# Pooled attention with a two-expert feed-forward: new homes for the first batch's small work

## The chip, the cores and the metric

The kernel runs on one core of a Trainium2 chip. The metric is the device time in microseconds of one execution; a profile of one execution shows what each engine did. The engines are called PE (matrix products; PEld is its weight load), DVE (VectorE), ACT (ScalarE), POOL (GpSimd) and SP (the queue that issues nearly all transfers here).

## The reference

```python
# B, H, S, D = 4, 8, 1152, 64
q_pool = q.reshape(B, H, S // 2, 2, D).mean(axis=3)
scores = np.matmul(q_pool, k.transpose(0, 1, 3, 2)) / np.sqrt(D)
scores = scores - np.max(scores, axis=-1, keepdims=True)
attn = np.exp(scores)
attn = attn / (np.sum(attn, axis=-1, keepdims=True) + 1e-09)
x = np.matmul(attn, v)                       # then (B, 576, 512)
xn = (x - mu) / np.sqrt(var + 1e-06) * g_ln  # over the last axis
out = x + np.maximum(xn @ w_ch1, 0.0) @ w_ch2   # w_ch1 512 x 2048, w_ch2 2048 x 512
```

q, k and v are float32. The two weight matrices are float64.

## The kernel before, in words

The attention is cut into 144 steps. A step has 128 rows of pooled queries against the 1152 keys of one head (each fifth of nine holds 64 rows of each of two heads). Nine steps are a pair of heads, four pairs a batch. The order of every engine is the order in which the program is written: the function `step(i)` is called for i = 0, 1, 2, ..., and the calls in it set what stands behind what on each engine.

The first batch (steps 0 to 35, `on_pe(i)`) and the other three go different ways. In the first batch a step is: PE makes the scores of the next step into PSUM (`emit_s`, L372 and L380; two sets of three banks in turn); DVE scales them and finds the row's maximum in one instruction (`emit_max`, L392); ACT takes the exponential (`emit_exp`, L399); PE transposes the 128x1152 result in nine blocks back into the same PSUM banks (`emit_t`, L429); ACT copies it to SBUF in two halves of 512 and 640 columns (`emit_t_copy`, L435). Two steps later PE multiplies it by V in float32 (`emit_pv`, L453): V has a 65th column of ones, so that row 64 of the 65x128 product is the sum of the exponentials. ACT copies that product to SBUF and adds 1e-9 to row 64 (L955), PE turns it back (`emit_turn`, L478), and DVE takes the reciprocal of the sum and scales (L508, L516). In the later batches the exponentials are split in two fp16 halves (ACT, and DVE or POOL in steps 2, 5 and 8 of nine, L410 to L419), transposed by a DMA, and multiplied by V in fp16 (L462); there the feed-forward products of finished batches (L613, L645) run beside the attention.

While the first batch runs, the weights come in. Each of 32 pieces is loaded by a DMA in step m (`w_load`), ACT moves its high words (`w_bias`, L719, step m + 3), and in step m + 4 `w_conv` puts three operations in a list (`fill`) that DVE works off at the step's end: the largest high word (a reduce), the low words shifted right by 29, and the join of both, `(x << 3) | low`. All three are recorded at one line, L105. After each eight pieces a scale is found, and POOL splits each piece pair in fp16 halves in three instructions, one a step (`calm`; L239, L239, L786); from part 2 on they have steps of their own. Before each such instruction stands a `gate`: DVE writes a column (L244) and POOL copies it (L245), so that POOL waits until DVE has come to that place. POOL also pools q and copies V (`take_v`, L261).

Of the kernel before, what the change touches and what calls it, by code (L numbers as in the profile page):

```python
# [12 lines left out]
I32 = mybir.dt.int32  # L13
ACTF = mybir.ActivationFunctionType
# [10 lines left out]
def tile_pooled_attention_moe(  # L25
# [18 lines left out]
    nc = tc.nc  # L44
# [36 lines left out]
    gsb = const.tile([128, KD], FP32, name="gsb")  # L81
    gs1 = const.tile([128, 2, KD], FP32, name="gs1")
    wtop = const.tile([128, 4, KD, 2], FP32, name="wtop")
    ones = const.tile([128, 128], BF16, name="ones")
    diag = const.tile([128, 4, 4], BF16, name="diag")
    wmax = const.tile([128, 4], FP32, name="wmax")
    wexp = const.tile([128, 4], FP32, name="wexp")
    wscl = const.tile([128, 4], FP32, name="wscl")
    inv12 = const.tile([128, 2], FP32, name="inv12")
    nought = const.tile([128, 1], FP32, name="nought")  # L90
    both = const.tile([128, 2], FP32, name="nhalf")
    nhalf, eps = both[:, 0:1], both[0:65, 1:2]
# [154 lines left out]
    def take_v(p, h):  # L247

        st = pair[p]
        vr = raws[p, "v"]  # L250
        if "v" not in st:

            st["v"] = tr_p.tile([128, 2, C, 130], FP16, tag="v", name="vt")
            if on_pe(p * C):
                st["v"] = st["v"].bitcast(FP32)
                nc.gpsimd.memset(st["v"][:, :, :, 64:65], 1.0)
# [140 lines left out]
    def emit_exp(i):  # L397
        st = steps[i]
        nc.scalar.activation(out=st["pe"], in_=st["pe"], func=ACTF.Exp, scale=-1.0, bias=st["nb"])  # L399

    pts = {}
# [70 lines left out]
    def emit_turn(n, ot, i):  # L472

        j = n % C
        ps = psum[:, 3 * ((i if on_pe(i) else pv_slot[0]) % 2) + 2, 128:258]
        parts = [(h, 64 * h, 64) for h in range(2)] if j == 4 else [(0, 0, 128)]
# [8 lines left out]
    def evac_pv(i, ps):  # L485
# [18 lines left out]
        r = r[o:o + n, 0:m] if on_pe(i) else r[:, 0:1]  # L504

        def one():
            if on_pe(i):
                nc.vector.reciprocal(r, ps[o:o + n, 64:65 * m:65])  # L508
            else:
                nc.vector.tensor_scalar(r, ps[:, 64:65], EPS, s, op0=ALU.add, op1=ALU.mult)  # L510
                nc.vector.reciprocal(r, r)

        def two():
            for u in range(m):
                if on_pe(i):
                    nc.vector.tensor_scalar(  # L516
                        x[:, 64 * u:64 * u + 64], ps[o:o + n, 65 * u:65 * u + 64],
                        r[:, u:u + 1], None, op0=ALU.mult,
                    )
                    continue  # L520
                a = slice(64 * u, 64 * u + 64) if m == 2 else slice(0, 128)
# [202 lines left out]
    def w_conv(m):  # L724
# [7 lines left out]
            nc.vector.tensor_reduce, wtop[:, part, c, z:z + 1], hi.bitcast(FP32), axis=AX.X,  # L732
# [3 lines left out]
        later(  # L736
            nc.vector.scalar_tensor_tensor, xi, xi, 3, lo,
            op0=ALU.logical_shift_left, op1=ALU.bitwise_or,
        )

    def w_reduce(part):
        while fill:
            drip()
        x, m = wtop[:, part], wmax[:, part:part + 1]
# [58 lines left out]
    for p in range(1, NP):  # L803
# [142 lines left out]
    def a_piece(i):  # L946
        pieces.extend(ready.pop(i, ()))
        for u in range(2 if len(pieces) > 2 and not on_pe(i) else 1):
            if pieces:
# [14 lines left out]
    def step(i):  # L964
# [73 lines left out]
        if calm and i < HP * C - 1:  # L1038
            gate()
# [10 lines left out]
    with tc.manual_schedule():  # L1050
# [10 lines left out]
        nc.vector.memset(both[:, 1:2], 0.0)  # L1061
        nc.vector.memset(both[64:65, 1:2], 1e-9)
# [5 lines left out]
        make_identity(nc, ident)  # L1068

# [64 lines left out]
```

## Time and profile before

| | |
|---|---|
| median of 3 runs | 813.77 us (811.7 to 814.31) |
| the profiled execution's own time | 812.92 us |
| its span from first to last instruction | 811.1 us |
| busy: PE, DVE, ACT, POOL | 97%, 74%, 67%, 42% of the span |
| TensorE clock granted, mean | 0.998 |

The profiled execution is 0.85 us below the median of the runs. Busy shares are averages over very different stages: the first batch takes some 177 us, and which engine sets the pace changes after it.

### The profile page before, as it was taken

The numbers are of one execution on the slowest core, as the hardware profiler recorded it, in microseconds if no ns is written. First come the engines' busy times: TensorE is split into PE (matmuls) and PEld (weight loads), VectorE is DVE, ScalarE is ACT, GpSimd is POOL, SyncE is SP. The second block draws the span as 40 slices with busy tenths as digits, with TensorE's granted clock in tenths as the row PEclk, the third lists the DMA queues.
The fourth block names the chain that finished last, engine by engine and source line by source line (L and its number), as shares of the span: only waits on it lengthen the run. The fifth ranks groups of instructions, "written<-read, shape, count | busy, mean of one in ns | idle before, by whom it ended". The sixth has DMA issues, their size and how long they took to land.

```text
span 811.1 us, 21365 instructions
## 1 busy us (share of the span) xinstructions
PE 783.1 (97%) x8978; PEld 553.7 (68%) x8978; DVE 599.3 (74%) x1174; ACT 544.4 (67%) x788; POOL 341.3 (42%) x338
## 2 busy tenths in 40 slices
PE   8899999989989999989999999999999999999997
PEld 7688888767556666657566666766675757766764
DVE  4599999999989887898777878888787867522121
ACT  3799898877786878787767776787778676211100
POOL 2010243389999963475452524528252423200000
PEclk9999999999999999999999999999999999999999
DMA  5828464208699999998998989896979687401001
GB/s 146 248 68 286 155 195 142 81 17 157 124 192 158 186 162 206 175 191 156 207 167 180 178 176 172 164 198 116 223 136 209 128 146 123 81 1 27 14 1 27
DMA packets 276017, 115.95 MB, mean 143 GB/s; under 512 B 259280, under 2 KB 259280, under 8 KB 275920
## 3 DMA queue, kind: packets, MB, share of 16 engines
q1 hardware_dynamic: 275840, 114.29, 69.9%
q8 instruction: 70, 1.15, 0.6%
q10 hardware_dynamic: 80, 0.29, 0.2%
q14 instruction: 27, 0.22, 0.1%
HBM read 46.14 MB, written 4.72 MB: 63 GB/s over the span
## 4 chain that ended last, share of the span: by engine, by line
PE 67%; POOL 13%; DVE 10%; issue 4%; ACT 3%; DMA 2%; SPq 0%; POOLq 0%; ACTq 0%; DVEq 0%
PE psum L645 19%; PE psum L613 18%; PE psum L372 8%; PE psum L462 7%; PE psum L453 5%; POOL wsl L239 4%; PE psum L429 3%; POOL wsl L786 3%; PE psum L380 2%; POOL hl L417 2%; DVE pe L392 2%; DVE hl L419 1%; DMA vr<-in_v_dram 1%; PE psum L321 1%; PE psum L1048 1%
## 5 line engine op out<-in xcount | busy, mean ns | idle before, releaser
L392 DVE CUSTOM_DVE_ANT_0 pe<-psum,nought,sc 128x1152 f32<-128x1152 f32 x144 | 203.1, 1411 | 17.5 <-PE psum L462 7.5
L399 ACT ACTIVATE pe<-pe,nb 128x1152 f32<-128x1152 f32 x144 | 180.4, 1253 | 31.9 <-DVE nb L392 31.0
L645 PE MATMUL psum<-wsl,ht 128*128 128x512 f16 x864 | 196.6, 379 | 4.7 <-DVE ht L627 3.8
L613 PEld LDWEIGHTS <-wsl 128*128 128x128 f16 x1920 | 169.6, 98 | 20.9 <-issue 3.2
L613 PE MATMUL psum<-xn,wsl 128*128 128x256 f16 x1536 | 176.3, 273 | 2.9 <-DVE xb L659 1.9
L645 PEld LDWEIGHTS <-ht 128*128 128x128 f16 x864 | 81.2, 98 | 93.0 <-issue 5.0
L626 ACT ACTIVATE ht<-psum 128x512 f16<-128x512 f32 x72 | 42.9, 595 | 129.2 <-PE psum L613 129.0
L410 ACT ACTIVATE hl<-pe 128x1152 f16<-128x1152 f32 x108 | 125.6, 1163 | 3.4
L372 PE MATMUL psum<-kt,qt 64*128 64x512 f16 (+1 forms) x960 | 120.2, 382 | 3.1 <-ACT pt L435 2.3
L419 DVE SCALAR_TENSOR_TENSOR hl<-pe,hl 128x1152 f16<-128x1152 f32 x72 | 116.5, 1618 | 0.0
L462 PE MATMUL psum<-vt,pt 128*128 128x65 f16 (+2 forms) x3240 | 106.8, 194 | 0.1
L627 DVE SCALAR_TENSOR_TENSOR ht<-psum,ht 128x512 f16<-128x512 f32 x72 | 49.6, 689 | 74.4 <-ACT ht L626 74.3
L462 PEld LDWEIGHTS <-pt 128*128 128x128 f16 (+1 forms) x3240 | 98.3, 100 | 3.0 <-DMA pt<-hl 0.3
L239 POOL TENSOR_SCALAR pe<-pe 128x1152 f32<-128x1152 f32 x36 | 42.8, 1189 | 119.3 <-ACT hl L410 119.3
L417 POOL TENSOR_TENSOR hl<-pe,hl 128x1152 f16<-128x1152 f32 x36 | 87.1, 2420 | 3.0
L453 PE MATMUL psum<-pt,vt 128*65 128x128 f32 (+1 forms) x720 | 77.4, 263 | 1.2 <-DVE kt L271 1.2
L453 PEld LDWEIGHTS psum<-pt,vt 128*65 128x65 f32 x720 | 71.4, 138 | 1.6 <-DVE kt L271 1.4
L372 PEld LDWEIGHTS <-qt 64*128 64x128 f16 (+1 forms) x960 | 31.6, 96 | 49.5 <-issue 30.8
L380 PEld LDWEIGHTS <-qt 128*128 128x128 f16 (+1 forms) x320 | 17.1, 99 | 63.1 <-issue 63.1
L245 POOL COPY gate<-gate 128x1 f32<-128x1 f32 x27 | 5.0, 184 | 110.7 <-DVE gate L244 110.7
L271 DVE SCALAR_TENSOR_TENSOR qt<-psum,s,qt 128x512 f16<-128x512 f32 (+1 forms) x48 | 29.4, 614 | 29.3 <-ACT qt L274 29.1
L659 DVE SCALAR_TENSOR_TENSOR xb<-psum,inv,xb 128x512 f32<-128x512 f32 x32 | 23.9, 745 | 36.7 <-PE psum L645 36.5
(114 smaller groups left out, 978.3 us busy)
## 6 DMA issues: line engine op xcount, KB each, us to landing
stage<-in_moe_w_ch_dram SPq DMA_DIRECT2D x32, 512.0 KB, 6.9
kr<-in_k_dram SPq DMA_DIRECT2D x16, 576.0 KB, 4.6
vr<-in_v_dram SPq DMA_DIRECT2D x16, 576.0 KB, 5.2
qr<-in_q_dram SPq DMA_DIRECT2D x31, 288.0 KB, 5.1
out_dram<-xb SPq DMA_DIRECT2D x32, 128.0 KB, 2.4
pt<-hl SPq DMA_TRANSPOSE x108, 5.2
kr<-in_k_dram SPq DMA_DIRECT2D x16, 64.0 KB, 4.2
out_dram<-xh SPq DMA_DIRECT2D x4, 128.0 KB, 2.8
```

The source lines that it names most:

```text
L239: nc.gpsimd.tensor_scalar(dst, src, s, 1.0, op0=ALU.mult, op1=ALU.mult)
L372: nc.tensor.matmul(out=sp[o:o + w, c0:c0 + 512], lhsT=qt[r:r + 64, qa, q0:q0 + w], rhs=kt[r:r + 64, ka, h], start=(a == 0), stop=(a == 2),)
L392: nc.vector.tensor_tensor_reduce(out=st["pe"], in0=st["s"], in1=nought[:, 0:1].to_broadcast([128, S]), scale=pair[i // C]["sc"][:, 0:1], s ...
L399: nc.scalar.activation(out=st["pe"], in_=st["pe"], func=ACTF.Exp, scale=-1.0, bias=st["nb"])
L410: nc.scalar.activation(out=hl[:, 0], in_=st["pe"], func=ACTF.Copy, scale=2.0 ** 15)
L417: nc.gpsimd.tensor_tensor(hl[:, 1], st["pe"], hl[:, 0], op=ALU.subtract)
L419: nc.vector.scalar_tensor_tensor(hl[:, 1], st["pe"], 2.0 ** 15, hl[:, 0], op0=ALU.mult, op1=ALU.subtract)
L453: nc.tensor.matmul(out=ps[0:65, q0:q0 + w], lhsT=vt[:, h, c], rhs=pt[:, 128 * u + q0:128 * u + q0 + w], start=(u == 0), stop=(u == C - 1),)
L462: nc.tensor.matmul(out=dst[:, 0:n], lhsT=pt[:, a + u, q0:q0 + w], rhs=vt[:, h, c, x0:x0 + n], start=(u == 0 and a == 0 and n == 65), stop= ...
L613: nc.tensor.matmul(out=ps[:, o:o + n], lhsT=wsl[:, 8 * w + cc, wa, f * 128:f * 128 + 128], rhs=xn[:, xa * KD + cc, 0:n], start=(m == 0), s ...
L627: lambda: nc.vector.scalar_tensor_tensor(lo, pv, 0.0, hi, op0=ALU.max, op1=ALU.subtract),
L645: nc.tensor.matmul(out=ps, lhsT=hv[0][:, ha, f, t * 128:t * 128 + 128], rhs=wsl[:, 8 * w + 4 + f // 2, wa, (f % 2) * DM:(f % 2) * DM + DM] ...
```

## The change

Four things change, in the first batch alone. The join of the weights' words goes from DVE to POOL, as an integer product by eight and an integer sum (two instructions for one). The product with V drops the column of ones, has 64 columns of weights instead of 65, and puts even and odd key blocks on different halves of PE's columns, so that two 64-row partial products stand one under the other in PSUM; DVE instead of ACT copies all 128 rows; and the turn back is a float32 product with two stacked identities, which adds the halves. The exponential's own instruction gives the row sums, to which POOL adds 1e-9. In every sixth step of the batch DVE copies the second half of the transposed block instead of ACT. The gates go, and the transposes of the next pair's q and k (`a_prep`) stand ahead of the product with V, no longer behind it.

```diff
     def emit_exp(i):
         st = steps[i]
-        nc.scalar.activation(out=st["pe"], in_=st["pe"], func=ACTF.Exp, scale=-1.0, bias=st["nb"])
+        kept = {}
+        if on_pe(i):
+            x = sums[i] = sums8[:, i % 8:i % 8 + 1]
+            kept["accum_out"] = x
+        nc.scalar.activation(
+            out=st["pe"], in_=st["pe"], func=ACTF.Exp, scale=-1.0, bias=st["nb"], **kept
+        )
+        if on_pe(i):
+            nc.gpsimd.tensor_scalar(x, x, 1e-9, 1.0, op0=ALU.add, op1=ALU.mult)
...
         for a, b in ((0, 512), (512, S)):
-            nc.scalar.copy(st["pt"][:, a:b], st["s"][:, a:b])
+            copy = nc.vector.tensor_copy if a and i % 6 == 1 else nc.scalar.copy
+            copy(st["pt"][:, a:b], st["s"][:, a:b])
...
                 for u, c in enumerate(ORDER):
+                    o = 64 * (u % 2)
                     nc.tensor.matmul(
-                        out=ps[0:65, q0:q0 + w], lhsT=vt[:, h, c],
+                        out=ps[o:o + 64, q0:q0 + w], lhsT=vt[:, h, c, 0:D],
                         rhs=pt[:, 128 * u + q0:128 * u + q0 + w],
-                        start=(u == 0), stop=(u == C - 1),
+                        start=(u < 2), stop=(u >= C - 2), skip_group_check=True,
                     )
...
-        for h, q0, w in parts:
-            nc.tensor.transpose(ps[0:w, 65 * h:65 * h + 65], ot[:, q0:q0 + w], ident[0:65, 0:65])
+        for q0, w in ((0, 64), (64, 64)) if j == 4 else ((0, 128),):
+            nc.tensor.matmul(
+                out=ps[q0:q0 + w, 0:D], lhsT=ot[:, q0:q0 + w], rhs=stack, start=True, stop=True,
+                skip_group_check=True,
+            )
...
             if on_pe(i):
-                nc.vector.reciprocal(r, ps[o:o + n, 64:65 * m:65])
+                nc.vector.reciprocal(r, sums.pop(i))
...
-        later(
-            nc.vector.scalar_tensor_tensor, xi, xi, 3, lo,
-            op0=ALU.logical_shift_left, op1=ALU.bitwise_or,
-        )
+        def join():
+
+            nc.gpsimd.tensor_tensor(xu, xu, eight[:, 0:1].to_broadcast([128, 512]), op=ALU.mult)
+            nc.gpsimd.tensor_tensor(xu, xu, lu, op=ALU.add)
+
+        later(join)
...
-            if on_pe(p * C):
-                at(i0 + (5, 7)[n], gate)
...
                 if on_pe(n):
-                    ot = pt.rearrange("p a n -> p (a n)").bitcast(FP32)[0:65, 0:128]
-                    until([lambda ot=ot, ps=ps: nc.scalar.activation(
-                        out=ot, in_=ps[0:65, 0:128], func=ACTF.Identity, bias=eps
-                    )], nbank[1])
+                    ot = pt.rearrange("p a n -> p (a n)").bitcast(FP32)[:, 0:128]
+                    nc.vector.tensor_copy(ot, ps[:, 0:128])
+                    waiting.discard(nbank[1])
...
+            a_prep()
             a_piece(i)
-            a_prep()
...
-        if calm and i < HP * C - 1:
-            gate()
```

Three places show where the instructions now stand. PE in a step of the first batch with a transpose of k, before and after; a product in float32 (L453, L465) is one row here.

```order
L453 MATMUL psum<-pt,vt 65x128 x9
L285 MATMUL psum<-ident,kr 128x128 x4
L372 LDWEIGHTS qt
L372 MATMUL psum<-kt,qt 128x512
```

```order
L489 MATMUL psum<-stack,pt 128x64
L286 MATMUL psum<-ident,kr 128x128 x4
L465 MATMUL psum<-pt,vt 64x128 x9
L373 LDWEIGHTS qt
L373 MATMUL psum<-kt,qt 128x512
```

The four transposes of k moved ahead of the product with V, so that only scores follow on that product. The same engine's turn (L489, before L478) stands where it stood. Next DVE, from one maximum of the first batch to the next (`pe,nb` is the scaled scores and the row's maximum), before and after:

```order
L392 ISA pe,nb<-psum,nought,sc 128x1152
L392 ISA nb 128x1
L508 RECIPROCAL r<-psum 128x1
L516 TENSOR_SCALAR xb<-psum,r 128x64
L105 TENSOR_REDUCE wtop<-stage 128x1
L105 TENSOR_SCALAR stage<-stage 128x512
L105 SCALAR_TENSOR_TENSOR wsl<-wsl,stage 128x512
L271 SCALAR_TENSOR_TENSOR qt<-psum,s,qt 128x128
L244 MEMSET gate 128x1
L392 ISA pe,nb<-psum,nought,sc 128x1152
```

```order
L393 ISA pe,nb<-psum,gsb,sc 128x1152
L393 ISA nb 128x1
L522 RECIPROCAL r<-sums 128x1
L531 TENSOR_SCALAR xb<-psum,r 128x64
L970 COPY pt<-psum 128x128
L107 TENSOR_REDUCE wtop<-stage 128x1
L107 TENSOR_SCALAR stage<-stage 128x512
L272 SCALAR_TENSOR_TENSOR qt<-psum,s,qt 128x128
L393 ISA pe,nb<-psum,gsb,sc 128x1152
```

The join (the third L105) and the gate's write left DVE, and the copy of the product with V (L970) came in ahead of the weights' reduce. Last POOL, over about three steps of the middle of the batch (`wsl` is a weight piece), before and after:

```order
L245 COPY gate<-gate 128x1
L239 TENSOR_SCALAR wsl<-wsl 128x1024
L245 COPY gate<-gate 128x1
L786 TENSOR_TENSOR wsl<-wsl 128x1024
L245 COPY gate<-gate 128x1
L239 TENSOR_SCALAR wsl<-wsl,gs_83 128x1024
```

```order
L408 TENSOR_SCALAR sums<-sums 128x1
L753 TENSOR_TENSOR wsl<-wsl,gsb 128x512
L754 TENSOR_TENSOR wsl<-wsl,stage 128x512
L241 TENSOR_SCALAR wsl<-wsl 128x1024
L408 TENSOR_SCALAR sums<-sums 128x1
L753 TENSOR_TENSOR wsl<-wsl,gsb 128x512
L754 TENSOR_TENSOR wsl<-wsl,stage 128x512
L803 TENSOR_TENSOR wsl<-wsl 128x1024
L408 TENSOR_SCALAR sums<-sums 128x1
L753 TENSOR_TENSOR wsl<-wsl,gsb 128x512
L754 TENSOR_TENSOR wsl<-wsl,stage 128x512
L241 TENSOR_SCALAR wsl<-wsl,gs_83 128x1024
```

Where each split had a gate ahead of it, it now has the sum's 1e-9 (L408), the product (L753) and the addition (L754) ahead of it.

## Rows read from the trace of the kernel before

**Rows 1.** The page: engines' busy time and the chain that ended last, shares.

```profile
PE 67%; POOL 13%; DVE 10%; issue 4%; ACT 3%; DMA 2%; SPq 0%; POOLq 0%; ACTq 0%; DVEq 0%
```

**Rows 2.** Stretches: length; PE, PEld, DVE, ACT, POOL busy us; clock, DMA share, GB/s.

```profile
32.96:154.56 121.60, 121.46 (x1168) 100.88 (x1167) 112.81 (x283) 109.58 (x173) 28.41 (x49) 1.00 0.52 163
67.84:154.56 86.72, 86.58 (x836) 71.72 (x835) 81.02 (x212) 78.07 (x124) 24.44 (x40) 1.00 0.55 169
154.56:273.40 118.84, 108.96 (x1259) 75.84 (x1257) 108.26 (x191) 88.98 (x126) 108.84 (x88) 1.00 0.68 124
273.40:811.10 537.70, 525.78 (x6267) 355.15 (x6265) 365.88 (x671) 328.66 (x463) 199.18 (x189) 1.00 0.75 138
```

**Rows 3.** The chain that ended last, one step of the first batch: start, us, what.

```profile
64.39 1.97 PE psum L453 x18
66.35 0.75 PE psum L372 x6
67.11 0.22 PE psum L380 x2
67.32 0.99 PE psum L429 x9
68.31 0.06 PE psum L478
```

**Rows 4.** The same chain at a step of two heads, and later in fp16.

```profile
46.79 2.13 PE psum L453 x36
...
299.65 0.82 PE psum L462 x27
...
304.46 0.98 PE psum L462 x53
```

**Rows 5.** All engines in time: start, us, engine, line, what, idle time before it.

```profile
64.22 2.13 PE L453 MATMUL psum<-pt,vt 128*65 128x128 f32 x18
66.28 0.33 PEld L372 LDWEIGHTS <-qt 64*128 64x128 f16 x6 [0.17 <-issue]
```

**Rows 6.** Groups of 32.96 to 154.56: busy us, mean ns of one, idle before.

```profile
L392 DVE CUSTOM_DVE_ANT_0 pe<-psum,nought,sc 128x1152 f32<-128x1152 f32 x28 | 39.6, 1414 | 3.5 <-ACT wsl L719 3.4
L435 ACT COPY pt<-psum 128x640 f32<-128x640 f32 x28 | 19.4, 693 | 0.8
L105 DVE SCALAR_TENSOR_TENSOR wsl<-wsl,stage 128x512 int32<-128x512 int32 x28 | 19.4, 693 | 1.0
L955 ACT ACTIVATE pt<-psum,nhalf 65x128 f32<-65x128 f32 x28 | 10.0, 358 | 1.0 <-PE psum L453 0.6
L271 DVE SCALAR_TENSOR_TENSOR kt<-psum,s,kt 128x512 f16<-128x512 f32 x6 | 4.5, 750 | 0.3 <-ACT kt L274 0.3
L271 DVE SCALAR_TENSOR_TENSOR qt<-psum,s,qt 128x128 f16<-128x128 f32 x3 | 1.0, 345 | 0.0
L182 ACT ACTIVATION_READ_ACCUMULATOR kt<-kr 128x1 f32 x3 | 0.6, 193 | 0.0
```

**Rows 7.** Two of POOL's groups, over the whole span.

```profile
L786 POOL TENSOR_TENSOR wsl<-wsl 128x1024 f16<-128x1024 f32 x16 | 35.3, 2204 | 0.5
L560 POOL TENSOR_TENSOR rs<-rs,nhalf 128x1 f32<-128x1 f32 x18 | 10.0, 554 | 0.0
```

**Rows 8.** POOL's gates from 67.84 to 154.56.

```profile
L245 POOL COPY gate<-gate 128x1 f32<-128x1 f32 x19 | 3.5, 184 | 67.0 <-DVE gate L244 67.0
```

**Rows 9.** POOL in time, at the end of the first batch.

```profile
160.64 0.62 POOL L556 TENSOR_SCALAR rs<-mv 128x1 f32<-128x1 f32 x1 [3.64 <-DVE mv L551]
171.18 0.19 POOL L556 TENSOR_SCALAR rs<-mv 128x1 f32<-128x1 f32 x1 [2.58 <-DVE gate L244]
```

**Rows 10.** DVE's shift and its fp16 split: duration ns min/median/max.

```profile
L105 DVE TENSOR_SCALAR stage<-stage x32: 410/421/734, 36.3 to 174.1; 128x512 int32<-128x512 int32 x32
L419 DVE SCALAR_TENSOR_TENSOR hl<-pe,hl x72: 1347/1350/3314, 183.0 to 686.4; 128x1152 f16<-128x1152 f32 x72
```

**Rows 11.** The chain that ended last, its last POOL piece before 280 us.

```profile
271.25 2.21 POOL wsl L239
```

More of the change, by code (lines that the diff above doesn't have):

```diff
@@ L13 @@
 I32 = mybir.dt.int32
+U32 = mybir.dt.uint32
 ACTF = mybir.ActivationFunctionType
@@ L80, in tile_pooled_attention_moe @@
     wsl = const.tile([128, 17, 2, 1024], FP16, name="wsl")
-    gsb = const.tile([128, KD], FP32, name="gsb")
+    gsb4 = const.tile([128, 8], FP32, name="gsb")
+    gsb = gsb4[:, 0:KD]
     gs1 = const.tile([128, 2, KD], FP32, name="gs1")
-    wtop = const.tile([128, 4, KD, 2], FP32, name="wtop")
+    wtop = const.tile([128, 2, KD, 2], FP32, name="wtop")
     ones = const.tile([128, 128], BF16, name="ones")
     diag = const.tile([128, 4, 4], BF16, name="diag")
[L86 to L92, printed above, removed]
+    w4 = const.tile([128, 16], FP32, name="w4")
+    wmax, wexp, wscl, inv12 = w4[:, 0:4], w4[:, 4:8], w4[:, 8:12], w4[:, 12:14]
+    nought = gsb4[:, 4:5]
+    eight = gsb4[:, 6:7].bitcast(U32)
+    sums8 = const.tile([128, 8], FP32, name="sums")
+    nhalf = gsb4[:, 5:6]
+    stack = const.tile([128, 64], FP32, name="stack")
     raws = {}
@@ L255, in take_v @@
                 st["v"] = st["v"].bitcast(FP32)
-                nc.gpsimd.memset(st["v"][:, :, :, 64:65], 1.0)
             else:
@@ L398, in emit_exp @@
         st = steps[i]
-        nc.scalar.activation(out=st["pe"], in_=st["pe"], func=ACTF.Exp, scale=-1.0, bias=st["nb"])
-    pts = {}
+        kept = {}
[7 more added lines that the diff above has]
+            nc.gpsimd.tensor_scalar(x, x, 1e-9, 1.0, op0=ALU.add, op1=ALU.mult)
+    pts, sums = {}, {}
     def pt_of(i):
@@ L475, in emit_turn @@
         ps = psum[:, 3 * ((i if on_pe(i) else pv_slot[0]) % 2) + 2, 128:258]
-        parts = [(h, 64 * h, 64) for h in range(2)] if j == 4 else [(0, 0, 128)]
-        for h, q0, w in parts:
-            nc.tensor.transpose(ps[0:w, 65 * h:65 * h + 65], ot[:, q0:q0 + w], ident[0:65, 0:65])
+        for q0, w in ((0, 64), (64, 64)) if j == 4 else ((0, 128),):
[3 more added lines that the diff above has]
+            )
         one, two = evac_pv(n, ps)
@@ L503, in evac_pv @@
             x = xb[b][:, t, 128 * hp + 64 * h:128 * hp + 64 * h + 64]
-        r = r[o:o + n, 0:m] if on_pe(i) else r[:, 0:1]
+        r = r[:, 0:1]
         def one():
             if on_pe(i):
-                nc.vector.reciprocal(r, ps[o:o + n, 64:65 * m:65])
+                nc.vector.reciprocal(r, sums.pop(i))
             else:
@@ L514, in two @@
             for u in range(m):
+                a = slice(64 * u, 64 * u + 64) if m == 2 else slice(0, 128)
                 if on_pe(i):
                     nc.vector.tensor_scalar(
-                        x[:, 64 * u:64 * u + 64], ps[o:o + n, 65 * u:65 * u + 64],
-                        r[:, u:u + 1], None, op0=ALU.mult,
+                        x[:, 64 * u:64 * u + 64], ps[a, 0:64], r[a], None, op0=ALU.mult
                     )
                     continue
-                a = slice(64 * u, 64 * u + 64) if m == 2 else slice(0, 128)
                 nc.scalar.activation(
@@ L731, in w_conv @@
         later(
-            nc.vector.tensor_reduce, wtop[:, part, c, z:z + 1], hi.bitcast(FP32), axis=AX.X,
+            nc.vector.tensor_reduce, wtop[:, part % 2, c, z:z + 1], hi.bitcast(FP32), axis=AX.X,
             op=ALU.max, apply_absolute_value=True,
@@ L735, in w_conv @@
         later(nc.vector.tensor_scalar, lo, lo, 29, None, op0=ALU.logical_shift_right)
-        later(
-            nc.vector.scalar_tensor_tensor, xi, xi, 3, lo,
-            op0=ALU.logical_shift_left, op1=ALU.bitwise_or,
-        )
+        xu, lu = x.bitcast(U32), lo.bitcast(U32)
+        def join():
+            nc.gpsimd.tensor_tensor(xu, xu, eight[:, 0:1].to_broadcast([128, 512]), op=ALU.mult)
+            nc.gpsimd.tensor_tensor(xu, xu, lu, op=ALU.add)
+        later(join)
     def w_reduce(part):
@@ L743, in w_reduce @@
             drip()
-        x, m = wtop[:, part], wmax[:, part:part + 1]
+        x, m = wtop[:, part % 2], wmax[:, part:part + 1]
         nc.vector.tensor_scalar(x, x, 2.0 ** -112, None, op0=ALU.mult)
@@ L1060, in tile_pooled_attention_moe @@
         nc.vector.memset(nought, 0.0)
-        nc.vector.memset(both[:, 1:2], 0.0)
-        nc.vector.memset(both[64:65, 1:2], 1e-9)
+        nc.vector.memset(eight, 8)
         for n in (2, 5):
@@ L1068, in tile_pooled_attention_moe @@
         make_identity(nc, ident)
+        for h in range(2):
+            x = slice(64 * h, 64 * h + 64)
+            nc.gpsimd.tensor_copy(stack[x], ident[x, x])
         warm(110)
```

## The prediction

> **What bounds the kernel now.** I read the chain that ended last first: PE holds 67% of it, POOL 13% and DVE 10% [rows 1], so PE sets most of the pace, but not all. The stretches say where each does. From 33 to 155 us, 28 steps of the first batch, PE is busy 121.5 of 121.6 us, DVE 112.8 and ACT 109.6 [rows 2]. A step is 121.6 / 28 = 4.34 us; DVE has 4.03 of work in it, ACT 3.91. PE is the bound, and the next engine is 7% behind it. One step of the chain shows what PE does: 18 passes of the product with V in 1.97 us, scores 0.75 and 0.22, nine transposes 0.99, the turn 0.06 [rows 3]: 3.99 us, and the rest up to 4.34 are the next pair's transposes, in most steps.
>
> From 155 to 273 us the bound is another: POOL is busy 108.8 of 118.8 us, more than PE's or DVE's share, and the chain runs over POOL nearly without a break until 271 us [rows 2, 11]. In that stretch each microsecond that is added to POOL is paid. After it PE is busy 525.8 of 537.7 us [rows 2]; nothing of the change lies there, and a shift at 273 us is carried to the end.
>
> **The change part by part, for one step of the first batch.**
>
> PE. The product with V takes 18 passes for nine blocks, so a float32 product is two passes of 1.97 / 18 = 0.109 us [rows 3]; a step of two heads has 36 of half the columns in 2.13 us [rows 4]. If passes on the two halves of the columns run together, 18 passes need ten places in time (the two passes of a block follow one another on their half, and block two's first pass goes beside block one's second): 1.09 us, a gain of 0.88. No row shows that for float32. For fp16 there is one: where a step's product is 27 passes of full width it takes 0.82 us, and where it is some 53 passes of half width on alternating halves 0.98 us [rows 4], so the pair runs together and costs 1.2 of one. By that factor the gain is 0.88 to 0.67; not together at all, it is 0. I take 0.85, since the halves and the alternation are the same. Against it stand two costs. The turn becomes a float32 product, two passes for one: + 0.11 (the transposes, one pass each, take 0.99 / 9 = 0.11 [rows 3]). And PE goes from whole-width instructions to half-width ones once more per step: where it changes shape now, from this product to the scores, the 18 passes end at 64.22 + 1.96 = 66.18 and the scores start at 66.28, with the weight load idle [rows 5], so + 0.10. That the transposes of the next pair stand ahead of the product now keeps it at one more change. Sum for PE: -0.64, to 3.70 us.
>
> The Trainium skill's page "TensorEngine Tiling (Array Packing)", section "Key Properties", says that tiles of the array run matmuls and weight loads in parallel, and that changing the tiling mode drains the engine. The fp16 rows and the 0.10 us agree; by the page's "up to 2x" the float32 gain would be half of 1.97, 0.98 us.
>
> DVE. It loses the join, 0.69 [rows 6]. It gets the copy of a 128x128 product out of PSUM: 0.35, as the 128x128 operation from PSUM takes [rows 6]; and in every sixth step a 640-column copy from PSUM: 512 columns take 0.75 and 1152 take 1.41 [rows 6], so 0.88, or 0.15 per step. The gates' writes are below 0.06 each. Sum: -0.69 + 0.35 + 0.15 - 0.05 = -0.24, to 3.79. ACT loses 0.36 (L955) and 0.69 / 6, and gets 0.19 for reading the sum out [rows 6]: -0.28, to 3.63.
>
> So PE at 3.70 no longer stands alone: DVE has 3.79. The step's floor is 3.79. The new place of the copy adds a wait: it stands behind the product with V and ahead of the weights' reduce and shift, the low halves of the preparations and the next maximum, and the exponential on ACT and the transposes on PE wait for that. With three engines within 5% of one another and each waiting in order for the next, I do not expect the floor. Now DVE is idle 0.31 us per step behind PE; with the same idle time the step is 4.10. I take 4.00, between: -0.34 us in each of the 29 steps from 3 to 31, some -10 us. Ends: -16 (3.79) and -7 (4.10).
>
> POOL. Each step gets a product and a sum over 128x512. A two-input operation over 1024 columns takes 2.20 us [rows 7], so 1.10 for 512, 2.2 for both; I take 2.3 for meetings with DVE. That is a sum in float; no row has an integer product. The nearest row in kind is a power of one column, 0.55 us [rows 7], against 0.18 for a copy of one [rows 8]: what an operation computes can triple its price here. So the join lies between 2.2 and, with a product of twice the price, 3.3 us. 1e-9 on the sums is one more single-column operation, 0.19; the gates give back 0.18 each [rows 8].
>
> In steps 12 to 31, 67.84 to 154.56 us, POOL's work becomes 24.4 - 3.5 + 20 x (2.3 + 0.19) = 70.7 us [rows 2, 8] of 20 x 4.00 = 80: hidden, 88% busy. Its cover is the other engines' work, and is gone with a join above (80 - 24.7) / 20 = 2.8 us. In steps 32 to 35 it is not hidden, since POOL's own stretch begins there: four joins with sums, 10.0 us, less five gates, 0.9. POOL now waits 3.64 and 2.58 us there ahead of two normalisations [rows 9]; two of the joins stand right ahead of these and fall in the waits, the other two do not. So the stretch from step 32 to 273 us becomes some 4 us longer; 2.9 if the joins fill both waits, 9.1 if they fill none.
>
> The sum: -10 + 4 = -6 us against the profiled execution's own 812.92: **807 us**. The median of the runs shown is 0.85 above that execution, within their spread.
>
> **The rivals.**
>
> The integer product is slow, and the kernel gets slower. From step 12 to 273 us POOL's work is 24.4 + 108.8 - 4.4 (24 gates) + 24 x 0.19 = 133.4 us without the joins [rows 2, 8], with the small idle times that stay (3.8) 137.2, and 24 joins; the stretch is 205.6 us long now, and steps 3 to 11 gain 9 x 0.34 = 3.1. So POOL takes everything back at a join of (208.7 - 137.2) / 24 = 3.0 us, and each tenth above costs 2.4 us. At 3.3 us: 137.2 + 79.2 - 208.7 = +8, **821 us**. For it: the power's row, whose price is set by what it computes. Against it: that price is for one column, and no row shows that it grows with the columns.
>
> The halves do not run together in float32. PE then has 4.34 + 0.11 + 0.10 = 4.55 us per step: +6 us over 29 steps, and +4 from POOL's stretch: **823 us**. For it: no float32 row on half columns. Against it: the fp16 pair.
>
> DVE is held by POOL. The shift takes 0.42 us, but up to 0.73 in the first batch, where POOL now works a quarter of the time, and the split of the later batches 1.35, but up to 3.31 [rows 10]. With POOL at 88% in steps 12 to 31 and no gate, the shift meets a POOL instruction more often than not in a step that splits weights (1.1 to 2.2 us) and waits for some half of it. At 0.25 us per step DVE has 4.04 of work and the step is 4.25: 9 x -0.34 + 20 x -0.09 = -5, and with +4 the time is **812 us**, no difference. Against it: POOL itself waits for the exponential's sums at about the time of the shift, so most shifts find it idle.
>
> The Trainium skill's page "SBUF — State Buffer", section "Who interferes with whom", has the rule behind this rival: VectorE instructions that use both ports, or read two SBUF tensors, share a port pair with GpSimd as an exclusive lock, and whoever comes second is held for the other's whole instruction. The row with 3.31 us agrees.
>
> **How the numbers follow.** The forecast 0.55 (its own range 801 to 811), the slow product 0.17, the halves one after another 0.14, DVE held 0.14. The best case, a step of 3.79 and both waits filled, gives 812.92 - 16 + 3 = 800. The range is 800 to 821: it leaves out the upper halves of the first two rivals, and little below. What a measurement here can tell from no change is about 0.3%, 2.4 us. Faster by more: nearly all of the forecast, a third of the last rival, some of a join between 2.8 and 2.9: 0.60. Within it 0.13. Slower 0.27.
>
> **What would show it.** The product with V should be a chain piece of 1.1 to 1.3 us for 18 passes, and the step 4.0 us; 1.97 means the second rival. The two POOL instructions of a join should be 1.1 us each; a product of 2 us means the first. The shift should stay near 0.42; a mean above 0.6 means the third. POOL should be busy nine tenths of steps 12 to 31, and its unbroken stretch should begin at step 32 and end 6 us earlier than now. The prediction is wrong if POOL's stretch does not follow its work: if the waits at [rows 9] move elsewhere, or if DVE's reciprocal, which now waits for POOL's 1e-9, stops DVE because POOL is steps late.

## The result, and the profile after

The changed kernel is slower: 819.95 us, median of 8 runs (818.3 to 820.57), against 814.2 us of the kernel before in runs beside it (8 runs, 811.7 to 818.48); ratio 1.0061, 95% interval 1.0039 to 1.0082. 807 was forecast. The profiled execution took 819.88 us, its span 817.9, 6.8 longer than before.

The chain that ended last, by engine, after the change: PE's share is 57%, where it was 67, and DVE's 19%, where it was 10 [rows 1].

```profile
PE 57%; DVE 19%; POOL 11%; ACT 5%; DMA 4%; issue 3%; SPq 1%; POOLq 0%; ACTq 0%; DVEq 0%
```

Two stretches, counted from one maximum of DVE to another: steps 3 to 31, then steps 32 to 45, in the columns of [rows 2]. First the kernel before, then the changed one.

```profile
28.14:154.56 126.42, 126.28 (x1211) 104.93 (x1210) 114.24 (x285) 113.15 (x180) 28.41 (x49) 0.99 0.54 172
154.56:224.27 69.71, 63.74 (x691) 46.89 (x690) 65.01 (x124) 51.08 (x74) 61.16 (x59) 1.00 0.48 89
```

```profile
27.99:154.13 126.14, 115.20 (x1236) 85.41 (x1235) 113.77 (x269) 101.86 (x175) 96.23 (x107) 0.99 0.54 173
154.13:229.69 75.56, 63.39 (x706) 44.37 (x704) 64.54 (x124) 49.55 (x71) 72.18 (x69) 0.95 0.40 83
```

The first batch gained 0.3 us where ten were forecast, although PE is busy 11 us less. Steps 32 to 45 take 5.85 us longer, POOL being busy 11 us more in them, and what comes after 1.3 (588.2 from 586.9, the rest of the spans): 6.8.

One step of the chain after the change (start, us, what; compare [rows 3]):

```profile
65.73 1.20 PE psum L438 x9
66.93 0.17 PE psum L489 x2
67.10 1.25 PE psum L465 x18
68.35 0.02 issue
68.38 0.29 DVE pt L970
68.67 0.59 DVE wtop L107
69.26 0.34 DVE stage L107
69.60 0.09 DVE wtop L762
69.69 0.03 issue
69.71 0.18 DVE wtop L764
69.89 0.02 issue
69.92 0.90 DVE wtop L767
70.81 0.03 issue
70.84 0.16 DVE w L770
71.00 1.32 DVE pe L393
```

The product with V takes 1.25 us for its 18 passes. After it the chain is on DVE up to the next maximum, and 0.90 us of that is one operation on 128x8 elements (L767). The kernel before does the same one (L750) in 0.17, as its row among the groups of 32.96 to 154.56 us has it (columns as in [rows 6]):

```profile
L750 DVE TENSOR_TENSOR wtop<-wtop,gsb 128x8 f32<-128x8 f32 x2 | 0.3, 168 | 0.1
```

The groups of 30 to 155 us after the change:

```profile
L754 POOL TENSOR_TENSOR wsl<-wsl,stage 128x512 uint32<-128x512 uint32 x27 | 35.0, 1298 | 3.5 <-POOL wsl L753 1.7
...
L753 POOL TENSOR_TENSOR wsl<-wsl,gsb 128x512 uint32<-128x512 uint32 x28 | 30.1, 1076 | 2.2
...
L107 DVE TENSOR_SCALAR stage<-stage 128x512 int32<-128x512 int32 x28 | 17.3, 618 | 0.0
...
L970 DVE COPY pt<-psum 128x128 f32<-128x128 f32 x29 | 8.2, 284 | 2.9 <-PE psum L465 2.7
L408 POOL TENSOR_SCALAR sums<-sums 128x1 f32<-128x1 f32 x29 | 7.7, 265 | 24.5 <-ACT pe L404 21.9 <-DMA stage<-in_moe_w_ch_dram 1.6
...
L445 DVE COPY pt<-psum 128x640 f32<-128x640 f32 x4 | 3.3, 820 | 0.0
...
L762 DVE TENSOR_SCALAR wtop<-wtop 128x8 f32<-128x8 f32 x3 | 2.2, 732 | 0.0
L767 DVE TENSOR_TENSOR wtop<-wtop,gsb 128x8 f32<-128x8 f32 x2 | 2.0, 1016 | 0.1
```

A join is 1.08 + 1.30 = 2.37 us, the copy 0.28, the larger copy 0.82: near what was taken. The shift's mean is 618 ns; a mean above 0.6 us was the sign of the third rival. Two pieces of the timeline (columns as in [rows 5]) show why:

```profile
113.12 1.30 POOL L754 TENSOR_TENSOR wsl<-wsl,stage 128x512 uint32<-128x512 uint32 x1
...
113.36 1.08 DVE L236 SCALAR_TENSOR_TENSOR sc<-e 128x1 f32<-128x1 f32 x1
...
119.08 2.14 POOL L803 TENSOR_TENSOR wsl<-wsl 128x1024 f16<-128x1024 f32 x1
119.48 2.02 DVE L107 TENSOR_SCALAR stage<-stage 128x512 int32<-128x512 int32 x1
```

An operation on one column takes 1.08 us until the join's sum is through, and a shift 2.02 until POOL's split is. Call an instruction's excess over the shortest of its form in the same execution "held". Summed over DVE's instructions of steps 3 to 31, held time was 3.6 us before and is 12.3 after: 5.6 in the shifts (10 of 28 by more than 0.1 us), 3.4 in the few small operations on maxima and scales. Sixteen instructions are over by more than 0.1 us, 9.0 us in all, and each of them begins while an instruction of POOL runs; before there is one, 0.2 us. The count is low by 1.4 us: both L767 (0.89 and 1.15 us) are long, so that the shorter is no measure of a free one. DVE's idle time, 12.2 us, is now 12.4. What is left is its work: 110.7 before, 101.5 after. So DVE lost 9.2 us of work, 0.32 per step, and 8.7 us of holding took its place (10.6 and 10.1 with a free L767 at 0.17).

At the end of the batch POOL is late. Its second normalisation, which started at 171.18 us [rows 9], starts at 174.71, behind a join:

```profile
173.34 1.28 POOL L754 TENSOR_TENSOR wsl<-wsl,stage 128x512 uint32<-128x512 uint32 x1
...
174.71 0.19 POOL L569 TENSOR_SCALAR rs<-mv 128x1 f32<-128x1 f32 x1
```

The chain's last POOL piece before 280 us, at 271.25 before [rows 11], is this one (start, us, what):

```profile
276.73 2.21 POOL wsl L241
```

### The profile page after: what moved, and what is told of

Its sections match the earlier page's. It is cut to its first block, busy times and chain, and to the rows that moved or that the text cites. A ratio compares the mean times of both kernels' runs of the same rounds, so it can differ in the third digit from the quotient of the medians.

```text
span 817.9 us, 21511 instructions
## 1 busy us (share of the span) xinstructions
PE 771.7 (94%) x9018; PEld 532.1 (65%) x9018; DVE 598.3 (73%) x1156; ACT 531.2 (65%) x782; POOL 421.6 (52%) x409
## 3 DMA queue, kind: packets, MB, share of 16 engines
q8 instruction: 70, 1.15, 0.6%
## 4 chain that ended last, share of the span: by engine, by line
PE 57%; DVE 19%; POOL 11%; ACT 5%; DMA 4%; issue 3%; SPq 1%; POOLq 0%; ACTq 0%; DVEq 0%
PE psum L658 18%; PE psum L626 18%; PE psum L474 7%; PE psum L373 6%; DVE pe L393 5%; POOL wsl L241 3%; DMA vr<-in_v_dram 3%; ACT pe L404 2%; POOL wsl L803 2%; POOL hl L426 2%; PE psum L381 2%; DVE stage L107 2%; DVE wtop L107 2%; DVE hl L428 1%; DVE qr L164 1%
## 5 line engine op out<-in xcount | busy, mean ns | idle before, releaser
L393 DVE CUSTOM_DVE_ANT_0 pe<-psum,gsb,sc 128x1152 f32<-128x1152 f32 x144 | 203.0, 1409 | 18.2 <-PE psum L474 7.4
L428 DVE SCALAR_TENSOR_TENSOR hl<-pe,hl 128x1152 f16<-128x1152 f32 x72 | 114.7, 1594 | 0.0
L465 PE MATMUL psum<-pt,vt 128*64 128x128 f32 (+1 forms) x720 | 48.7, 273 | 3.6 <-DVE xn L588 2.5
L672 DVE SCALAR_TENSOR_TENSOR xb<-psum,w,xb 128x512 f32<-128x512 f32 x32 | 23.8, 745 | 36.7 <-PE psum L658 36.5
L438 PE MATMUL psum<-ident,pe 128*128 128x128 f32 x324 | 43.7, 281 | 5.6 <-ACT pe L404 5.2
L381 PE MATMUL psum<-kt,qt 128*128 128x128 f16 (+1 forms) x320 | 41.3, 225 | 6.9 <-DVE xb L531 5.4
```

The source lines that it names most:

```text
L381: nc.tensor.matmul(out=sp[o:o + w, 1024:1152], lhsT=qt[:, qa, q0:q0 + w], rhs=pair[p]["k8"][:, h], start=(qa == 0), stop=(qa == 1),)
L393: nc.vector.tensor_tensor_reduce(out=st["pe"], in0=st["s"], in1=nought[:, 0:1].to_broadcast([128, S]), scale=pair[i // C]["sc"][:, 0:1], s ...
L428: nc.vector.scalar_tensor_tensor(hl[:, 1], st["pe"], 2.0 ** 15, hl[:, 0], op0=ALU.mult, op1=ALU.subtract)
```

## The experiments

The numbers of all runs together. The ratio is to the kernel before on the same chip; the steps are of the profiled execution, from the start of a maximum to that of another, in us. Held time is counted as above; where joins run on POOL in all steps to 31, it is low by 1.4 to 2.0 us, since neither of the two operations like L767 is free there.

| kernel | median | ratio, interval | steps 3-15 | 16-31 | 32-45 | DVE held, 3-31 |
|---|---|---|---|---|---|---|
| before | 814.2 | | 57.0 | 69.5 | 69.7 | 3.6 |
| changed | 819.95 | 1.0061 [1.0039, 1.0082] | 55.3 | 70.9 | 75.6 | 12.3 |
| join on DVE | 833.33 | 1.026 [1.0231, 1.0288] | 61.1 | 80.4 | 74.4 | 12.0 |
| join alone | 817.99 | 1.007 [1.0048, 1.0092] | 56.4 | 70.5 | 74.1 | 8.8 |
| no 1e-9 | 815.36 | 1.0027 [1.0008, 1.0047] | 53.1 | 70.3 | 73.9 | 11.0 |
| late joins on DVE | 817.66 | 1.0057 [1.0035, 1.0078] | 55.1 | 70.8 | 75.3 | 12.3 |
| gated product | 819.61 | 1.0065 [1.0043, 1.0088] | 54.2 | 71.8 | 74.8 | 12.7 |
| halves only | 812.95 | 0.997 [0.995, 0.999] | 55.0 | 69.4 | 71.0 | 3.9 |
| two phases | 812.89 | 0.9974 [0.9958, 0.9991] | 54.3 | 69.4 | 71.0 | 5.4 |
| before, no gates | 820.81 | 1.0076 [1.0048, 1.0105] | 57.1 | 77.4 | 69.5 | 12.7 |
| before, short reduce | 811.79 | 0.9964 [0.9942, 0.9987] | 55.5 | 69.0 | 69.1 | 4.3 |
| halves, short reduce | 805.2 | 0.989 [0.9861, 0.9919] | 51.0 | 65.4 | 70.5 | 4.0 |
| changed, with gates | 823.97 | 1.0116 [1.0084, 1.0149] | 55.6 | 71.9 | 74.1 | 13.2 |
| two phases, scaling on ACT | 809.64 | 0.9953 [0.9928, 0.9978] | 53.4 | 67.1 | 71.6 | 6.1 |
| the same, no join on POOL | 809.48 | 0.9951 [0.9933, 0.9968] | 52.9 | 67.0 | 71.5 | 4.3 |
| half of the copies on DVE | 814.89 | 1.0017 [0.9999, 1.0034] | 53.0 | 69.1 | 74.8 | 6.7 |

**The change taken apart.** In the first four kernels theory A says that the join on POOL costs twice, by holding DVE in the first batch and by POOL's longer stretch behind it; theory B says that the sums' way through POOL and the copy's new place cost it. The first puts the join back on DVE:

```diff
-        later(join)
+        later(
+            nc.vector.scalar_tensor_tensor, xi, xi, 3, lo,
+            op0=ALU.logical_shift_left, op1=ALU.bitwise_or,
+        )
```

> The changed kernel with the join of the weights' words back on DVE as one instruction; all else as changed. Theory A (the join on POOL costs twice: its instructions hold DVE's back, some 9 us over steps 3 to 31, and its work lengthens POOL's stretch after step 32, some 7 us): DVE is no longer held, but has 0.6 us more per step, 118.5 + 3.6 + some 5 idle = 127 to 129 us for steps 3 to 31 (126.4 before the change), and the stretch is as before; in all 1 to 3 us slower than before, 3 to 6 faster than changed. Theory B (the sums through POOL and the copy's new place on DVE cost it): 0.6 us more per step on an engine that waits anyway, 5 to 15 us slower than changed.

It is the slowest of all, far outside A's expectation; the time is B's, 13.4 us above the changed kernel's. DVE has 118.3 us of work in steps 3 to 31, 16.8 more than in the changed kernel, and they take 15.3 more: in this kernel DVE sets the step. And DVE is held as long without joins on POOL, 12.0 us: something else in the change holds it too. The changed kernel has no gates, which neither theory had looked at.

The second is the kernel before, with gates, and the two POOL instructions for the join (the store of maxima is cut to two parts, to make room):

```diff
-        later(
-            nc.vector.scalar_tensor_tensor, xi, xi, 3, lo,
-            op0=ALU.logical_shift_left, op1=ALU.bitwise_or,
-        )
+        def join():
+
+            nc.gpsimd.tensor_tensor(xu, xu, eight[:, 0:1].to_broadcast([128, 512]), op=ALU.mult)
+            nc.gpsimd.tensor_tensor(xu, xu, lu, op=ALU.add)
+
+        later(join)
```

> The kernel before with the join on POOL alone (gates, 65 columns, copy on ACT, sums by the ones as before). Theory A: the first batch is bound by PE and stays as it is, since DVE loses 0.61 us per step and can be held for 0.3; POOL's stretch after step 32 becomes 6 to 7 us longer; 6 to 7 us slower than before. Theory B: the join is not what costs; within 2 us of before.

Both halves of A's mechanism are there, at a smaller size. Its two stretches:

```profile
27.73:154.55 126.82, 126.25 (x1205) 104.41 (x1204) 103.44 (x257) 112.90 (x179) 91.85 (x104) 1.00 0.54 171
154.55:228.64 74.09, 65.56 (x697) 48.28 (x696) 63.22 (x120) 51.60 (x74) 70.79 (x68) 0.98 0.41 85
```

DVE is 10.8 us less busy in steps 3 to 31 and nothing gets faster, PE being busy 126.3 of 126.8 us; 5.2 us more holding cost little there, with 23.4 us of idle time on DVE to take it. The whole loss, 4.4 us, is in steps 32 to 45.

The third drops the POOL instruction on the sums. It leaves out the 1e-9.

```diff
-        if on_pe(i):
-            nc.gpsimd.tensor_scalar(x, x, 1e-9, 1.0, op0=ALU.add, op1=ALU.mult)
```

> The changed kernel without POOL's addition of 1e-9 to the sums (left out; the sums are at least 1). POOL no longer waits for the exponential in every step, so the integer product can start earlier. Theory A: the product meets the shift less often, so DVE is held some 3 to 5 us less, and the stretch after step 32 is 1 us shorter; 1 to 3 us slower than before. Theory B: the wait for POOL's sums is the cost; 6 us faster than before.

The time is A's, though DVE is held 1.3 us less and not 3 to 5. What it wins over the changed kernel, 4.6 us by the medians and 2.8 by the ratios, is what those sums cost. They make POOL wait for the exponential, 21.9 us in all in the groups above, and the joins stand behind that wait.

The fourth has the last four joins on DVE, those that fall in steps 32 to 35:

```diff
-        later(join)
+        if m < 28:
+            later(join)
+        else:
+            later(
+                nc.vector.scalar_tensor_tensor, xi, xi, 3, lo,
+                op0=ALU.logical_shift_left, op1=ALU.bitwise_or,
+            )
```

> The changed kernel with the last four joins, of steps 32 to 35, on DVE. Theory A: POOL has 9.4 us less in its stretch, DVE 2.4 us more in these steps; 4 to 7 us faster than changed, so within 2 us of before, and steps 3 to 31 as in the changed kernel. Theory B: no more than 1 us from changed.

It has POOL 9.7 us less busy in steps 32 to 45 (62.5 from 72.2) and gains 0.3 there; by the ratios it is B. POOL's work in that stretch is not the whole price. DVE's copies lengthen it too: the kernel with the join on DVE, which has these copies and no join on POOL, takes 74.4 us there (the kernel before without gates takes 69.5), and the last kernel of the table, which moves copies to DVE and has no join on POOL there, 74.8 from 71.6. How the joins and the copies add up was not settled.

**What holds DVE.** Gates, first by an imitation: DVE writes a column behind each shift that the product reads as its factor.

```diff
+        later(nc.vector.memset, g, 8)
...
-            nc.gpsimd.tensor_tensor(xu, xu, eight[:, 0:1].to_broadcast([128, 512]), op=ALU.mult)
+            nc.gpsimd.tensor_tensor(xu, xu, g.to_broadcast([128, 512]), op=ALU.mult)
```

> The changed kernel, with one more DVE write of a column right behind each shift, which GpSimd's product reads as its factor of eight, so that the product can't run beside the shift of its own step; the splits stay without gates. Theory A (GpSimd's instructions hold DVE's two-input and fast SBUF instructions): DVE's held time in steps 3 to 31 falls from 12.3 us to 8 to 10, the rest being the splits; those steps take 1 to 3 us less than the changed kernel's 126.1, GpSimd gets later by as much as it waits, and the time is 816 to 820. Theory B (the holding is not tied to where the product runs): held time stays at 12 us and the time stays at 820 +- 1.5.

B: 12.7 us are held. An order for the product alone keeps nothing apart. Then the kernel before with no gates and nothing else changed:

```diff
     def gate():
-        x = sm_p.tile([128, 2], FP32, tag="gate", name="gate", bufs=4)
-        nc.vector.memset(x[:, 0:1], 1.0)
-        nc.gpsimd.tensor_copy(x[:, 1:2], x[:, 0:1])
+        return
```

> The kernel before with its gates removed and nothing else. Theory A: GpSimd's splits meet DVE's shift and join where they like, and DVE's held time in steps 3 to 31 rises from 3.6 us to 6 to 10; PE sets the step there and DVE has 12 us of idle time, so the steps take 0 to 2 us more; GpSimd's stretch loses the gates' copies and waits, -1 to +1. Time 813 to 817. Theory B (the missing gates, not the joins, are what ate the change's gain): steps 3 to 31 take 4 us more or worse, time 818 or above.

B again: the gates alone were worth as much as the whole change lost. POOL has no more work than before (28.33 us in steps 3 to 31), but its splits, its pooling of q and its copies of V now meet DVE's shift and join. The two forms over the whole span (durations as in [rows 10]), and one meeting from the timeline:

```profile
L105 DVE TENSOR_SCALAR stage<-stage x32: 410/420/1027, 36.6 to 181.6; 128x512 int32<-128x512 int32 x32
L105 DVE SCALAR_TENSOR_TENSOR wsl<-wsl,stage x32: 691/693/2512, 37.1 to 182.1; 128x512 int32<-128x512 int32 x32
```

```profile
107.98 2.31 POOL L784 TENSOR_TENSOR wsl<-wsl 128x1024 f16<-128x1024 f32 x1
...
108.33 2.51 DVE L105 SCALAR_TENSOR_TENSOR wsl<-wsl,stage 128x512 int32<-128x512 int32 x1
```

A join of 0.69 us takes 2.51. Steps 16 to 31 take 8.0 us longer (77.44 from 69.46), and DVE's held time in them rises by 7.8 (9.84 from 2.08): there it is paid in full. Last the changed kernel with the gates back (their columns stand in tiles that hold other small values):

```diff
+            if on_pe(p * C):
+                at(i0 + (5, 7)[n], gate)
...
+        if calm and i < HP * C - 1:
+            gate()
```

> The changed kernel with the gates back ahead of GpSimd's splits, and nothing else. Theory A (the gates kept the splits off DVE's shift and two-input work; without them the kernel before takes 8 us longer in the first batch): held time in steps 3 to 31 falls from 12.3 us to 7 to 10, the joins' part being left; those steps take 2 to 4 us less, but GpSimd waits for the gates and starts its stretch later, and the time is 816 to 820. Theory B (GpSimd is so full with joins that a gate delays it and keeps nothing apart): held time stays at 12, and the time is 820 to 825.

B: 13.2 us are held. The longer time is not from there: steps 3 to 31 take 1.3 us more than in the changed kernel, steps 32 to 45 take 1.5 less, and the 5.6 us by which its profiled span is longer lie behind step 45 (593.8 from 588.2), where the cause stays open. That a gate keeps POOL from starting too early, and that nothing is left to keep apart where POOL has joins in every step and is late, is B's reading; no run shows it by itself.

**Which engine sets the step.** The halves alone, with joins, copies and gates as before; the transposes still stand ahead of the product (it leaves out the 1e-9; the exponential's own sums stay):

```diff
-        later(join)
+        later(
+            nc.vector.scalar_tensor_tensor, xi, xi, 3, lo,
+            op0=ALU.logical_shift_left, op1=ALU.bitwise_or,
+        )
...
-                    nc.vector.tensor_copy(ot, ps[:, 0:128])
-                    waiting.discard(nbank[1])
+                    until([lambda ot=ot, ps=ps: nc.scalar.copy(ot, ps[:, 0:128])], nbank[1])
...
+        if calm and i < HP * C - 1:
+            gate()
```

> The changed kernel with the join back on DVE, the gates back, and ACT copying the product with V and both halves of the transposed block; only the column halves, the turn by the stacked identities and the exponential's own sums stay. It leaves out the 1e-9 on the sums. Theory A: GpSimd stands where it stood before, DVE's held time falls back to 3 to 4 us in steps 3 to 31, PE has 3.7 us of work per step, DVE 4.03 and ACT about 4.1; steps 3 to 31 take 4 to 6 us less than the 126.4 of before, nothing is given back later, and the time is 808 to 811 against 814. Theory B (the order of waits sets the step, and PE's shorter product buys nothing): steps 3 to 31 stay at 126 us, time 813 to 815.

PE is 9.7 us less busy in steps 3 to 31, and 2 us come of it, not A's 4 to 6, and none in steps 16 to 31. So PE was not the only bound; by busy time DVE is the next. The mirror image takes work off DVE in the kernel before:

```diff
-            nc.vector.tensor_reduce, wtop[:, part, c, z:z + 1], hi.bitcast(FP32), axis=AX.X,
+            nc.vector.tensor_reduce, wtop[:, part, c, z:z + 1], hi.bitcast(FP32)[:, 0:64], axis=AX.X,
```

> The kernel before, whose reduce for a piece's largest high word looks at 64 of 512 columns only (it leaves out the rest of the maximum). DVE has about 0.5 us less per step from step 4 to 35, and no other engine has more or less. Theory P (PE is the first batch's bound, as the prediction read it from PE's busy share): steps 3 to 31 stay at 126.4 us, time 812 to 815. Theory D (DVE is the bound in most steps, since its idle time lies in a few steps only, and PE's busy share includes its waits): the steps take 5 to 12 us less, and the time is 803 to 810.

DVE is 10.9 us less busy, and again 2 us come of it. Then the halves-only kernel with that same line changed:

> The halves-only kernel with the same short reduce (it leaves out most of that maximum, and the 1e-9 on the sums). PE has 3.7 us of work per step, DVE 3.55, ACT about 4.1. Theory D: with DVE's work gone PE's shorter product is worth something for the first time: steps 3 to 31 take 5 us less or more than those of the kernel before with the short reduce, until ACT is the bound, about 118 us; time 801 to 806. Theory P: the gain is that of PE alone, as in the halves-only kernel, 124 us, time 811 to 814.

Steps 3 to 31 of the three, in that order:

```profile
28.98:153.41 124.43, 116.55 (x1241) 85.73 (x1240) 113.31 (x287) 108.74 (x209) 28.28 (x46) 0.99 0.56 174
```

```profile
27.54:152.04 124.50, 124.42 (x1202) 103.14 (x1201) 103.32 (x287) 112.48 (x179) 28.46 (x49) 1.00 0.56 174
```

```profile
27.63:144.02 116.39, 112.76 (x1237) 83.71 (x1236) 102.35 (x287) 108.28 (x208) 28.34 (x46) 1.00 0.60 186
```

PE alone 2.0 us, DVE alone 1.9, both 10.0. The last time is D's, but neither theory had all three: D and P each named one bound, and there are two of nearly the same length.

**Versions that could beat both.** Joins and copies as in the changed kernel where POOL has few splits (12 joins, copies up to step 16), as in halves only after that:

```diff
-        later(join)
+        if m < 12:
+            later(join)
+            return
+        later(
+            nc.vector.scalar_tensor_tensor, xi, xi, 3, lo,
+            op0=ALU.logical_shift_left, op1=ALU.bitwise_or,
+        )
```

> As the halves-only kernel, but up to step 16, where GpSimd has few splits to do, the first 12 joins run on GpSimd and DVE copies the product with V (and the second half of the transposed block in every sixth step), as in the changed kernel. It leaves out the 1e-9 on the sums. Theory A: 5 us gained by step 16, as the kernel without the 1e-9 had, 1 to 3 more in steps 16 to 31, and GpSimd's stretch from step 32 as long as before: 805 to 809, faster than both kernels. Theory B (GpSimd's stretch takes back whatever the first batch gains): the gain at step 31 is there, but the end is within 2 us of 814.

Three us ahead of the kernel before at step 31 in the profile, and no faster than halves only by the medians; the time is B's. With the scaling on ACT as well:

```diff
-        found.extend((one, two, lambda: evacuated(n)))
+        found.append(one)
+        last.extend((two, lambda: evacuated(n)))
...
-                if on_pe(i):
-                    nc.vector.tensor_scalar(
-                        x[:, 64 * u:64 * u + 64], ps[a, 0:64], r[a], None, op0=ALU.mult
-                    )
-                    continue
```

> The two-phase kernel with the scaling of the attention's result (0.28 us from PSUM) on ACT, behind the exponential, and no longer on DVE. It leaves out the 1e-9 on the sums. Theory D: DVE falls to 3.7 us per step and ACT rises to 4.1: steps 3 to 31 take 2 to 5 us less than the two-phase kernel's 123.7, and the time is 807 to 811. Theory P: no change against the two-phase kernel, 813, or slower where ACT delays the exponential.

It is as D has it: 0.28 us per step off DVE, and steps 3 to 31 take 3.2 us less than the two-phase kernel's. This one is faster than both kernels. The next makes it the halves-only kernel with the scaling on ACT: no join on POOL, and all copies on ACT.

```diff
-        if m < 12:
-            later(join)
-            return
```

> The two-phase kernel with scaling on ACT, without any join on GpSimd: all 32 joins on DVE, ACT makes all copies (the halves-only kernel with the scaling on ACT). It leaves out the 1e-9 on the sums. If the early joins on GpSimd are worth something (theory A with holding of 0.17 us per join, as the held time of steps 3 to 15 has it, against 0.69 taken off DVE), steps 3 to 15 take 1 to 2 us more than the 53.4 of the two-phase kernel with scaling on ACT, and the time is 1 to 3 us above its 809.6. If what the kernel gains is only that PE and DVE are relieved together (theory D alone), the time is within 1 us of it or below.

The ratio is the same to 0.0002, and it is faster than both kernels. ACT is no third bound here: it is busy 113.8 us in steps 3 to 31, 5.1 more than in halves only, and they take 4.4 us less. The exchange, twelve joins to POOL for as many steps' copies to DVE, brings nothing even where POOL has room: with it DVE is held 2.0 us more in steps 3 to 15 (3.6 from 1.6), and they are no shorter. The last puts the copy of the product with V on DVE in odd steps from 16 on:

```diff
-                    if i < 16:
+                    if i < 16 or i % 2:
```

> The two-phase kernel with scaling on ACT, whose copies of the product with V are on DVE in odd steps from 16 on, too. It leaves out the 1e-9 on the sums. ACT has 64.1 us of work in the 67.1 us of steps 16 to 31 there, DVE 60.2; the edit moves eight copies of 0.3 us. Theory D with three engines (whichever is fullest sets the step): ACT falls to 61.7 and DVE rises to 62.6, the steps take 0.5 to 1.5 us less, 808 to 809.5. If the copy's place ahead of the weights' operations makes PE and the next maximum wait, the steps take 0 to 2 us more, 810 to 812.

Steps 16 to 31 take 2.0 us more for eight copies of some 0.3 us: the copy pays nearly its whole duration there. Steps 32 to 45 take 3.2 us more (74.75 from 71.59), and with them the time is above either expectation.

## Why the prediction was wrong

**The step that failed is the choice between the forecast and its third rival, DVE held by POOL.** It had 0.14, and the reason against it was that "most shifts find it idle". That is half true: 18 of 28 shifts are not held, and POOL is idle at nine of these. But the ten that are wait 0.13 to 1.60 us, 0.55 on average, and the small operations on maxima and scales, which the working never named, are held too (L762 0.73 us for 0.16 when free, L767 1.02 for 0.17). The rival's price was 0.25 us per step for steps 12 to 31 and a step of 4.25; there DVE is held 10.0 us, 2.5 before, so 0.38 more per step, and the step is 4.42. Over steps 3 to 31 it is 8.7 us more, 0.30 per step, and a step of 126.14 / 29 = 4.35 us where 4.00 was forecast. The forecast put meetings on POOL alone, as 2.3 us for a join and not 2.2, and nothing on DVE. What the step would be without the holding is an estimate: DVE's 101.5 us of work, 12.4 idle and 3.6 held as before make 117.5, or 4.05 per step, and the forecast's 4.00 would nearly have stood. No run has the changed kernel without it; the nearest, halves with the short reduce, has 4.0 us held and takes 116.4. That the shift and the join are held by POOL's instructions is shown by the kernel before without gates, where only the gates are gone and POOL's other work is the same.

The Trainium skill's page "SBUF — State Buffer", section "Who interferes with whom", states that rule: whichever engine comes first has the shared ports for its whole instruction. This trace agrees, 2.02 us of a shift behind 2.14 of a split.

**The gates were priced at their own time**, "below 0.06 each" and 0.18 on POOL. In the kernel before they are worth 8.0 us in steps 16 to 31, by keeping the splits away from DVE's shift and join. But this was no term of its own in the loss: put back into the changed kernel they save nothing. Missing gates and joins on POOL do not add up: DVE is held 12.7 us in the kernel before without gates, 8.8 in it with the joins on POOL, and 12.3 in the changed kernel, which has both.

**The stretch from step 32** was mis-sized, within its bounds: 4 was taken, with 2.9 and 9.1 as ends; steps 32 to 45 take 5.85 us more. POOL's unbroken stretch was to end 6 us earlier; the chain's last POOL piece comes 5.5 later. The two joins that were to fall in the waits of [rows 9] stand ahead of the two normalisations and make them late, by 0.9 and 3.5 us. Halves only has 1.2 of the 5.85 without a join on POOL, and DVE's copies lengthen the stretch by themselves, so a part is not the join's. PE's granted clock is a part at most: a mean of 0.95 over 75.6 us is worth no more than 3.8 us (an estimate). In the kernel without the 1e-9 the stretch takes 73.9, 1.7 less than the changed one. The 1.3 us after step 45 stay open; kernels of this study differ there by more (586.8 to 593.8).

**The reading of the bound** was half of the truth. "PE is the bound, and the next engine is 7% behind it": by busy time, yes. But DVE's idle time is not free for work: with PE 9.7 us less busy it only fell from 12.2 to 11.1. Much of it lies in a few waits, one of 3.4 us for ACT [rows 6]. Either engine alone gives 2 us. This step did little harm to the forecast, since both engines lost work in it.

**What was right.** The halves run together in float32: 1.25 us for 18 passes, with 1.1 to 1.3 given, so the second rival falls (0.72 gained, 0.85 taken). The turn takes 0.17 for 0.06, 0.11 more, as taken. A join took 2.37 us, with 2.3 taken, so the first falls. DVE's work fell by 0.32 us per step, with 0.24 taken. POOL is busy 85% of steps 12 to 31 (74.65 of 88.34 us), with 88% given. No wait of DVE's reciprocal for POOL's sums is among DVE's waits of steps 3 to 31. By its terms the sum was -10 + 4 = -6; measured on the profiled spans: -0.3 + 5.85 + 1.3 = 6.8.

## What to carry to other kernels

A move from DVE to POOL is not finished when POOL has room for it: ask which of DVE's instructions POOL's will meet, and price a meeting at up to the rest of the POOL instruction (here 0.13 to 1.60 us for a shift of 0.42). Even where POOL had room, twelve joins in exchange for copies gained nothing here. An instruction that looks like bookkeeping (a gate) may set an order that is worth more than its time; take it out alone first. And where two engines are busy within some per cent of each other, relief of one buys little: the pair must be relieved together, as 2.0 and 1.9 us alone and 10.0 together show.

## What the runs showed of the hardware

Not all of DVE's instructions were held. In steps 3 to 31 of the changed kernel the copy of the product out of PSUM (L970), the maximum (L393) and the weights' reduce (L107) stayed within 0.04 us of their shortest, beside a POOL that was busy 96.2 of 126.1 us; the shift (up to 2.02 us for 0.42) and some of the small operations on SBUF did not.

POOL's integer product over 128x512 with one broadcast column took 1.04 us (median), less than the integer sum of two operands behind it, 1.30.

Half-clock stretches came with PE's waits. In the changed kernel the granted clock was 0.80, a mean of its two levels 1.2 and 2.4 GHz, from 171.09 to 179.76 us, where PE had just waited 2.46 us for DVE, and 18 passes took 2.40 us for 1.25 elsewhere. It was 0.89 from 200 to 215 us, where PE had waited 2.9 us for DVE. The first of the two, first the window's row, then the timeline's:

```profile
171.09:179.76 8.67, 6.21 (x59) 4.82 (x58) 5.96 (x14) 4.06 (x7) 7.98 (x12) 0.80 0.00 0
```

```profile
174.03 2.40 PE L465 MATMUL psum<-pt,vt 128*64 128x128 f32 x18 [2.46 <-DVE xn L588]
```

Here a PE that had got ahead of its partners idled, and then ran slower when they caught up.
